# Moving small reciprocals from VectorE to GpSimd, and two small VectorE operations one place later, in a top-32 attention with mixture of depths

## The chip, the cores and the metric

The kernel runs on one core of a Trainium2 chip. The metric is the device time in microseconds (us) of one execution; a core has five engines with queues of their own: PE (TensorE), DVE (VectorE), ACT (ScalarE), POOL (GpSimd) and SP (SyncE, here only DMA).

## The reference

Inputs q, k and v are float32 of shape (8, 8, 576, 64): batch, heads, rows, width. The mixture has w_gate (512), w1 (512 x 1024), w2 (1024 x 512) and a capacity of 128. Cut to what matters:

```python
scores = (q @ k.T) / 8                                # 576 x 576 for each batch and head
kth    = 32nd largest score of each row
scores = where(scores >= kth, scores, -1e9)
e      = exp(scores - row max)
x      = (e / (sum(e) + 1e-9)) @ v                    # heads side by side: (8, 576, 512)
s      = x @ w_gate                                   # one gate a token
top    = the 128 tokens of a batch with the largest s
ye     = relu(x[top] @ w1) @ w2
out    = x;  out[top] += ye / (1 + exp(-s[top]))
```

## The kernel before, in words

**Units and steps.** The work is cut into 144 units, 18 for each of the 8 batches. A unit is a tile of 128 query rows for two heads (four tiles of four units a batch), or the last 64 rows for four heads (two units a batch). One loop, `for n in range(-1, N)` at L1192, runs all units as a pipeline: in step n the scores of unit n+1 are multiplied, the search of unit n is begun, that of unit n-2 ended, and unit n-4 is weighed and multiplied by v. Everything is recorded through `InOrder` (L38 to L46), so each engine executes in the order of the program text, and the profile gives L46 as the line of nearly all instructions; tiles tell them apart.

**The 32nd score.** ACT copies the scores from PSUM to the tile `sc`. DVE takes the eight largest of each of seven pieces of a row into `cand` (`find_bound`, L544: 14 MAX8 a step, for two heads), and from these candidates the 24th (`best`, `bound`). ACT takes the signs of score minus bound (`sides`, L578), POOL multiplies score by sign (`y<-sc,sides`, L1160, two a step), and DVE takes the eight largest of that (`next<-y`, `find_kth`, L598); the last of them is the 32nd. `mask` (L603) marks the smaller scores in `less`: head 0 by ACT, head 1 by POOL. PE transposes scores and marks together, ACT takes the exponential (`pT`, `last`), PE multiplies by v and a column of ones, and ACT copies the result to `xs`, and the sums plus 1e-9 to `sums` (`keep_sums`, L735).

**Dividing by the sums.** In the step after a tile's last unit, `normalise` (L730) calls `divide` (L738). DVE takes the reciprocal of 8 sums of a row into `rden`, and POOL multiplies `xs` by it into `x`. The call is put at the front of `vector_late` (L1225), which `find_bound` empties between the two heads (L552). So DVE has the reciprocal between its 7th and its 8th MAX8 of `cand`, and POOL has the multiplication between its mask of that step and the two `y` of that step. One step later DVE takes the dot product with w_gate (`dot`, L1028). There are 40 tiles; the very last is divided by lines of its own (L1447).

**The mixture.** `mixture` (L786) is a generator, whose pieces run in chosen steps of the next batch (`mix_at`, L1072). `multiply_places` finds the chosen tokens by PE; `add_up` (L895) adds parts (`place`), makes row numbers (`row_i`, by `keep_rows`) and the gates (`g`), all by DVE at the end of a step, out of the list `after_kth`. A POOL DMA fetches the rows in the next step. ACT takes exp(-g), and `squash` (L906) makes 1/(1+g) by two DVE instructions, out of `vector_late`. ACT uses `g` much later, in `gy`. `keep_least` (L1174) takes the least 32nd score of a batch by a DVE reduction of `next`, recorded in the step that follows the batch's last `find_kth`, ahead of that step's MAX8.

**What sets the order.** Lists of closures: `late` and `copies_late` for ACT, `vector_late` and `amid_late` for DVE, `pool_late` for POOL (emptied after `find_bound`, L1307), `after_kth` for DVE after `find_kth`. The last units have a hand-written order from L1335 on. `general` (L1655) and `general_weights` are a slower way for other inputs, taken only where `is_unsure` is set, and the profiled execution does not run them.

Of the kernel before, what the change touches and what calls it, by code (L numbers as in the profile page):

```python
# [11 lines left out]
ALU = mybir.AluOpType  # L12
FP32 = mybir.dt.float32
# [36 lines left out]
def kernel(  # L50
# [11 lines left out]
    nc = tc.nc  # L62
    P = nc.NUM_PARTITIONS
    B, H, S, D = q.shape
# [14 lines left out]
    const = ctx.enter_context(tc.tile_pool(name="const", bufs=1))  # L79
# [3 lines left out]
    wkpool = ctx.enter_context(tc.tile_pool(name="wk", bufs=2))  # L83
# [3 lines left out]
    modpool = ctx.enter_context(tc.tile_pool(name="mod", bufs=1))  # L87
# [32 lines left out]
    for i in range(2):  # L120
# [22 lines left out]
    least = const.tile([P, B], FP32, name="least")  # L143
    bounded = const.tile([P, NS], FP32, name="bounded")
    sums = const.tile([P, B * NT, H], FP32, name="sums")
    nc.gpsimd.memset(sums, 1.0)

    MIDDLE = S - 2 * (TOP_K - 8) + 1
    steps_i = const.tile([P, 2, 8], I32, name="steps_i")
# [16 lines left out]
        out=slot_signs,  # L166
        in0=slot,
        scalar1=-2.0,
        scalar2=float(S - 1),
        op0=ALU.mult,  # L170
# [22 lines left out]
    def load_weights():  # L193
# [6 lines left out]
    pe, dve, act, pool, sp = (  # L200
        InOrder(tc, e)
        for e in (nc.tensor, nc.vector, nc.scalar, nc.gpsimd, nc.sync)
    )
# [16 lines left out]
    late, vector_late, pool_late = [], [], []  # L220
# [3 lines left out]

    kept, values_bank = [], [None]

    after_kth = []

    def flush_copies():
        while copies_late:  # L230
# [2 lines left out]
    def flush():  # L233
        flush_copies()
        while late:
            late.pop(0)()
# [307 lines left out]
    def find_bound(sc, bound):  # L544

        cand = wkpool.tile([P, 2, 8 * PARTS], FP32, name="cand")
        best = [stats.tile([P, 2, 8], FP32, name=f"best{r}") for r in range(2)]
        best.append(bound)
        for i in range(2):

            if i == 1:
                flush_vector()  # L552
            for u in range(PARTS):
                if (i, u) == (1, 2) and amid_late:
                    amid_late.pop()()
                dve.max(
                    cand[:, i, 8 * u : 8 * u + 8],
                    sc[:, i, u * S // PARTS : (u + 1) * S // PARTS],
                )


        parts = cand.rearrange("p i (u e) -> p i u e", u=PARTS)
        for r, e in enumerate((3, 7, 8)):
            for i in range(2):
                dve.max(best[r][:, i, :], parts[:, i, :, 0:e])
            if r < 2:
                for i in range(2):
                    dve.match_replace(
                        parts[:, i, :, 0:e],
                        best[r][:, i, :],  # L570
                        parts[:, i, :, 0:e],
                        LOWEST,
                    )
# [163 lines left out]

    def divide(n, xs, x, den):  # L738
        rden = stats.tile([P, H], FP32, name="rden")
        dve.reciprocal(out=rden[0:n, :], in_=den)  # L740
        pool.tensor_tensor(
            x.rearrange("p (h d) -> p h d", h=H),
            xs[0:n, :, 0:D],
            rden[0:n, :].unsqueeze(2).to_broadcast([n, H, D]),
            ALU.mult,
        )
# [39 lines left out]
    def mixture(row0, pg, rank, exact=False, sign_sum=None):  # L786
# [8 lines left out]
        if exact:  # L795
            for t0, t1, at in ((0, J, 0), (J, NT, JP)):
                tr = ps_misc.tile([P, 512], FP32, name="tr", tag="misc")
                n = R if t0 else P
# [8 lines left out]
        else:  # L807
            row_dram = drampool.tile([1, S], FP32, name="row_dram")
            sp.dma_start(
                out=row_dram[0, R * NT : S].rearrange("(p j) -> p j", j=J),  # L810
                in_=gate[R:P, 0:J],
            )
            sp.dma_start(
                out=row_dram[0, 0 : R * NT].rearrange("(p j) -> p j", j=NT),
                in_=gate[0:R, 0:NT],
# [18 lines left out]
        for t in range(NT):  # L834
            yield
            n = R if t == J else P
# [52 lines left out]
        g = modpool.tile([P, 1], FP32, name="g", bufs=2)  # L889
# [4 lines left out]

        def add_up():  # L895
            add_parts(place, found)
            keep_rows(
                place,
                row_i,
                row0 if isinstance(row0, float) else row0[:, 0:1],  # L900
                float(done * S - 1),
            )
            dve.tensor_scalar_max(out=g, in0=place[:, 1:2], scalar1=-88.0)
            late.append(lambda: act.activation(g, g, AF.Exp, scale=-1.0))

        def squash():  # L906
            dve.tensor_scalar_add(out=g, in0=g, scalar1=1.0)
            dve.reciprocal(out=g, in_=g)

        kept.append(lambda: after_kth.append(add_up))  # L910
        if exact:
            for todo in (kept, after_kth):
                while todo:
                    todo.pop(0)()
        yield
# [15 lines left out]
        for fc in range(NFC):  # L931
            yield
            if fc == 1:
                vector_late.append(squash)
            if fc % 2 == 0:
                ps = ps_misc.tile([P, 2, CAP], FP32, name="h_ps", tag="misc")
            multiply_h(ps[:, fc % 2, :], fc, xeT)
            if fc % 2 == 1:
                copies_late.append(
                    lambda ps=ps, fc=fc: act.activation(  # L940
                        hT[:, fc - 1 : fc + 1, :], ps, AF.Relu
                    )
                )
# [34 lines left out]
    def add_parts(place, found):  # L978
        dve.tensor_reduce(
            out=place,  # L980
            in_=found[:, 0:6].rearrange("p (a e) -> p a e", e=3),
            axis=mybir.AxisListType.X,
            op=ALU.add,
        )

    def keep_rows(ps, row_i, row0, most):

        dve.tensor_scalar(
            out=row_i,
            in0=ps[:, 0:1],  # L990
            scalar1=row0,
            scalar2=most,
            op0=ALU.add,
            op1=ALU.min,
        )
# [99 lines left out]
    for b in range(B - 1):  # L1095
        n = (b + 1) * per_batch + mix_at_of.get(b, mix_at)[6]
# [77 lines left out]
    def keep_least(b, bound, kth):  # L1174
        at = 2 * per_batch * b
        late.append(
            lambda: act.copy(
                out=bounded[:, at : at + 2 * per_batch].rearrange("p (n i) -> p n i", i=2),
                in_=bound,
            )  # L1180
        )
        dve.tensor_reduce(
            out=least[:, b : b + 1], in_=kth, axis=mybir.AxisListType.XY, op=ALU.min
        )

    def mask_of(n, on=None):
# [5 lines left out]
    for n in range(-1, N):  # L1192
        b, i = divmod(n, per_batch)
# [48 lines left out]
        if is_unit(n + 1):  # L1242
            b, t, g = units[n + 1]
# [15 lines left out]
        if is_unit(n + 1) and n + 1 >= NHP:  # L1259
            b, i = divmod(n, per_batch)  # L1260
# [56 lines left out]
        if gating is not None:  # L1317
            b, t = gating
# [10 lines left out]
        b, i = divmod(n, per_batch)  # L1329
# [117 lines left out]
    rden = stats.tile([P, H], FP32, name="rden")  # L1447
# [20 lines left out]
    for t in (0, 1):  # L1468
        pool.tensor_scalar(
            out=pick[:, t, :],  # L1470
            in0=slot,
            scalar1=rank[:, t : t + 1],
            scalar2=others[:, t : t + 1],
            op0=ALU.subtract,
# [8 lines left out]
    for t in (J - 1, J):  # L1483
        n = R if t == J else P
        dve.tensor_scalar(
            out=pick[0:n, t, :],
            in0=slot[0:n, :],
            scalar1=rank[0:n, t : t + 1],
            scalar2=others[0:n, t : t + 1],
            op0=ALU.subtract,  # L1490
# [5 lines left out]
    g = modpool.tile([P, 1], FP32, name="g", bufs=2)  # L1496
# [15 lines left out]
    for i in range(2):  # L1512
        dve.tensor_scalar(
            out=half_i[:, i : i + 1],
            in0=row_i,
            scalar1=2.0,
            scalar2=float(i),
            op0=ALU.mult,
# [10 lines left out]
    for copy, half, dc in zip((act.copy, dve.tensor_copy), halves, (0, 2)):  # L1529
        copy(  # L1530
            out=xeT[:, dc : dc + 2, :],
            in_=half[:, 0 : 2 * CAP].rearrange("p (c i) -> p c i", c=2),
        )

    keep_least(B - 1, bounds.pop(B - 1)[:, :, :, 7], next8s.pop(B - 1)[:, :, :, 7])
    flush()
    low = modpool.tile([P, S], I32, name="low", tag="scratch")[:, 0:NS]
    dve.tensor_scalar(
        out=low,
        in0=bounded.bitcast(I32),  # L1540
        scalar1=(1 << 23) - 1,
# [85 lines left out]
    def general_weights(sc):  # L1627

        p = wkpool.tile([P, 2, S], FP32, name="p", tag="y")
        for i in range(2):  # L1630
            cur, tops = sc[:, i, :], []
            left = wkpool.tile([P, 2, S], FP32, name="left", tag="y")
            for r in range(TOP_K // 8):
                tops.append(stats.tile([P, 8], FP32, name=f"top{r}", bufs=2))
                nc.vector.max(tops[-1], cur)
                if r < TOP_K // 8 - 1:
                    nc.vector.match_replace(left[:, 0, :], tops[-1], cur, LOWEST)
                    cur = left[:, 0, :]
            shift = stats.tile([P, 1], FP32, name="shift", bufs=2)
            nc.vector.tensor_scalar_mul(shift, tops[0][:, 0:1], -scale)  # L1640
            e = wkpool.tile([P, S], FP32, name="e", tag="sides")
            nc.scalar.activation(
                e, sc[:, i, :], AF.Exp, bias=shift, scale=scale
            )
            nc.vector.scalar_tensor_tensor(
                out=p[:, i, :],
                in0=sc[:, i, :],
                scalar=tops[-1][:, 7:8],
                in1=e,
                op0=ALU.is_ge,  # L1650
                op1=ALU.mult,
            )
        return p
# [77 lines left out]
```

## Time and profile before

| | |
|---|---|
| Median of 3 runs | 786.59 us (786.38 to 789.53) |
| The profiled execution | 788.9 us, of which 786.6 us from its first to its last instruction (the span) |
| Granted TensorE clock | 0.996 |
| Busy: PE, DVE, ACT, POOL | 725.7, 756.7, 731.3, 692.4 us |
| DVE RECIPROCAL of `rden` | 40, 188 ns each with 128 rows, 180 ns with 64 |
| DVE RECIPROCAL of `g` | 8, 164 ns each |
| POOL `x<-xs,rden` | 39, about 1.04 us each |
| DVE reductions of `next` to `least` | 8, 217 ns each |

"Busy" is time in which an engine has at least one instruction between its start and its end. On DVE the next instruction starts before the one in front of it has ended, so durations of small instructions, added up, give more than they occupy; the distance from one start to the next tells what one occupies. A wait is put down to the engine and the tile that released it last.

### The profile page before, as it was taken

To read this page: it belongs to the slowest core of one execution; us is meant where nothing else is said; L and a number is where in the kernel's file an instruction comes from. 1 tells how busy PE (TensorE), PEld (TensorE's weight loads), DVE (VectorE), ACT (ScalarE), POOL (GpSimd) and SP (SyncE) were. 2 spreads that over 40 slices of the span, in tenths; PEclk is the share of its full clock that TensorE was granted. 3 is DMA by queue.
4 is the path that set the end of the run, shared out by engine and by line. 5 is a ranking of instruction groups with operands and counts; after the bars stand their busy time and mean duration, and the time that the engine had idled before them with its cause. 6 is when DMAs were issued, how large, how long until landed. Compare 5 with 4: busy or idle time off the path is not lost. (4 is left out here: it accounts for less than half of the span.)

```text
span 786.6 us, 33176 instructions
## 1 busy us (share of the span) xinstructions
PE 725.7 (92%) x12535; PEld 550.5 (70%) x12535; DVE 756.7 (96%) x4602; ACT 731.3 (93%) x1535; POOL 692.4 (88%) x732
## 2 busy tenths in 40 slices
PE   8888888888999989999999999999899989999987
PEld 6766666666786668766786667866687658757756
DVE  7999999999999999999999999999999999999952
ACT  6999999999999999999999999999999999989730
POOL 3899999999999998999999999999999999999821
PEclk9999999999999999999999999999999999999899
DMA  8941215121151132321251221512233102101021
GB/s 168 293 105 39 48 56 111 30 55 30 62 118 35 38 94 54 76 57 42 70 110 31 56 43 63 114 26 50 65 77 82 30 15 70 25 15 17 2 75 31
DMA packets 121751, 50.69 MB, mean 64 GB/s; under 512 B 116016, under 2 KB 116016, under 8 KB 120560
## 3 DMA queue, kind: packets, MB, share of 16 engines
q1 hardware_dynamic: 118368, 43.94, 22.7%
q0 software_dynamic: 1744, 4.20, 3.0%
q8 instruction: 101, 1.65, 0.9%
q14 instruction: 66, 0.54, 0.2%
q10 hardware_dynamic: 1472, 0.36, 0.2%
HBM read 36.93 MB, written 11.55 MB: 62 GB/s over the span
## 5 line engine op out<-in xcount | busy, mean ns | idle before, releaser
L46 POOL TENSOR_TENSOR y<-sc,sides 128x576 f32<-128x576 f32 x288 | 349.8, 1237 | 24.8 <-ACT sides L46 23.3
L46 DVE MAX8 cand<-sc 128x8 f32<-128x82 f32 (+1 forms) x2016 | 313.1, 230 | 3.0 <-ACT sc L46 2.9
L46 POOL TENSOR_SCALAR less<-sc,next 128x576 bf16<-128x576 f32 x135 | 233.3, 1728 | 28.4 <-DVE next L46 23.8
L46 ACT ACTIVATE sides<-sc,bound 128x576 fp8e4<-128x576 f32 x288 | 230.9, 802 | 3.9 <-DVE bound L46 3.7
L46 PEld LDWEIGHTS av<-v,pT 128*64 128x64 f32 x4608 | 146.9, 138 | 87.2 <-ACT last L46 78.7
L46 DVE MAX8 next<-y 128x8 f32<-128x584 f32 x288 | 204.4, 751 | 0.0
L46 PE MATMUL av<-v,pT 128*64 128x65 f32 x4608 | 166.9, 225 | 35.0 <-ACT last L46 34.7
L46 PE MATMUL ps<-kT,qT 64*128 64x288 f32 (+1 forms) x1248 | 170.4, 422 | 2.9 <-ACT sc L46 2.1
L46 PEld LDWEIGHTS <-less 64*128 64x128 bf16 (+1 forms) x2448 | 161.2, 131 | 13.0 <-POOL less L46 10.0
L46 PE MATMUL ptr<-ident,sc 64*128 64x64 f32 x2272 | 161.5, 253 | 0.0
L46 ACT COPY sc<-ps 128x1152 f32<-128x1152 f32 x140 | 160.5, 1146 | 0.0
L46 ACT ACTIVATE pT<-ptr 128x1024 f32<-128x1024 f32 x142 | 147.3, 1037 | 10.1 <-PE ptr L46 9.3
L46 PEld LDWEIGHTS ptr<-ident,sc 64*128 64x128 f32 x2272 | 138.2, 137 | 23.8 <-issue 23.7
L46 PE MATMUL ptr<-out_of_reach,less 64*128 64x64 bf16 x2272 | 148.2, 190 | 6.3 <-POOL less L46 5.3
L46 ACT ACTIVATE less<-sc,next 128x576 bf16<-128x576 f32 x147 | 115.4, 789 | 0.0
L46 PEld LDWEIGHTS ps<-kT,qT 64*128 64x128 f32 (+1 forms) x1248 | 92.6, 176 | 22.6 <-ACT sc L46 5.1
L46 DVE MATCH_REPLACE8 cand<-best,cand 128x21 f32<-128x21 f32 (+1 forms) x576 | 99.0, 180 | 0.0
L46 DVE MAX8 best<-cand 128x8 f32<-128x21 f32 (+1 forms) x576 | 91.0, 191 | 0.0
L46 ACT ACTIVATION_READ_ACCUMULATOR sides<-sc,bound 128x1 f32 x288 | 63.6, 221 | 0.0
L46 PE MATMUL h_ps<-xeT,w 128*128 128x128 f32 x464 | 61.9, 278 | 0.0
L46 PEld LDWEIGHTS av<-ident,sc 128*128 128x128 f32 x144 | 20.0, 139 | 55.9 <-issue 40.9
L46 PE MATMUL av<-vpair,last 128*64 128x130 f32 x576 | 56.9, 276 | 0.0
(167 smaller groups left out, 916.2 us busy)
## 6 DMA issues: line engine op xcount, KB each, us to landing
v<-in_v_dram SPq DMA_DIRECT2D x64, 128.0 KB, 4.0
out_dram<-x SPq DMA_DIRECT2D x8, 1024.0 KB, 3.9
rows<-in_k_dram SPq DMA_DIRECT2D x56, 128.0 KB, 2.9
rows<-in_q_dram SPq DMA_DIRECT2D x56, 128.0 KB, 3.1
w<-in_moe_w_dram SPq DMA_DIRECT2D x2, 2048.0 KB
gate_row<-row_dram SPq DMA_DIRECT2D x7, 288.0 KB, 4.6
last<-in_q_dram SPq DMA_DIRECT2D x8, 128.0 KB, 3.5
vpair<-in_v_dram SPq DMA_DIRECT2D x16, 64.0 KB, 5.1
```

Of the source, the lines that this page charges most:

```text
L46: return lambda *a, **kw: self._tc.keep_in_program_order(fn(*a, **kw))
```

## The change

The 39 reciprocals of `divide` and the two operations of `squash` go from DVE to POOL, as a sum with an immediate and powers of -1, with a tile of -1 as the second operand. `squash` goes into `pool_late` and so runs after `find_bound` of the same step. The reduction in `keep_least` and, of `add_up`, all but the first addition go into a new list `after_max`, emptied after the first MAX8 of `cand` in the next `find_bound`: the same step's for the reduction, the next step's for row numbers and gates. The exponential of `g`, which `use_place` puts into `late`, runs one step later for that. A tile of the other way, `general_weights`, moves to another pool. The last tile's reciprocal (L1448) and the last batch's gate (L1509) stay on DVE.

```diff
+    minus_one = const.tile([P, H], FP32, name="minus_one")
+    nc.gpsimd.memset(minus_one, -1.0)
...
-    after_kth = []
+    after_kth, after_max = [], []
...
                     cand[:, i, 8 * u : 8 * u + 8],
                     sc[:, i, u * S // PARTS : (u + 1) * S // PARTS],
                 )
+                while after_max:
+                    after_max.pop(0)()
...
     def divide(n, xs, x, den):
         rden = stats.tile([P, H], FP32, name="rden")
-        dve.reciprocal(out=rden[0:n, :], in_=den)
+        pool.tensor_tensor(rden[0:n, :], den, minus_one[0:n, :], ALU.pow)
...
         def add_up():
             add_parts(place, found)
+            after_max.append(use_place)
+
+        def use_place():
             keep_rows(
...
         def squash():
-            dve.tensor_scalar_add(out=g, in0=g, scalar1=1.0)
-            dve.reciprocal(out=g, in_=g)
+            pool.tensor_scalar(
+                out=g, in0=g, scalar1=1.0, scalar2=None, op0=ALU.add
+            )
+            pool.tensor_tensor(g, g, minus_one[:, 0:1], ALU.pow)
...
-            for todo in (kept, after_kth):
+            for todo in (kept, after_kth, after_max):
...
             if fc == 1:
-                vector_late.append(squash)
+                pool_late.append(squash)
...
-        dve.tensor_reduce(
-            out=least[:, b : b + 1], in_=kth, axis=mybir.AxisListType.XY, op=ALU.min
+        after_max.append(
+            lambda: dve.tensor_reduce(
+                out=least[:, b : b + 1], in_=kth, axis=mybir.AxisListType.XY, op=ALU.min
+            )
         )
...
     keep_least(B - 1, bounds.pop(B - 1)[:, :, :, 7], next8s.pop(B - 1)[:, :, :, 7])
+    after_max.pop()()
...
-            e = wkpool.tile([P, S], FP32, name="e", tag="sides")
+            e = modpool.tile([P, S], FP32, name="e", tag="scratch")
```

## The prediction

> **What bounds the kernel now.** First the busy times of the page and of one batch in the middle of the loop (18 units), from a view of stretches: us, then the busy us of PE, PEld, DVE, ACT and POOL with instructions in brackets.
>
> ```profile
> PE 725.7 (92%) x12535; PEld 550.5 (70%) x12535; DVE 756.7 (96%) x4602; ACT 731.3 (93%) x1535; POOL 692.4 (88%) x732
> ...
> 100.00:745.00 645.00, 606.49 (x10726) 459.22 (x10724) 644.20 (x3944) 630.31 (x1318) 603.42 (x615) 1.00 0.24 55
> ...
> 398.00:490.30 92.30, 88.76 (x1557) 66.78 (x1555) 92.20 (x568) 91.28 (x193) 86.46 (x89) 1.00 0.27 63
> ```
>
> DVE has 0.10 us of idle time in a batch of 92.30 us: it bounds the loop, and the page's 96% comes from the two ends. But ACT has only 92.30 - 91.28 = 1.02 us left in a batch, POOL 92.30 - 86.46 = 5.84 us. A DVE saving counts as far as these two can follow. Who waits for whom in that batch (engine, tile, what it waits for; us in total, times, longest), for ACT and then POOL:
>
> ```profile
> ACT pT L46 <- PE ptr L46: 0.4, 1, 0.4
> ACT sides L46 <- DVE bound L46: 0.3, 1, 0.3
> ...
> POOL less L46 <- DVE next L46: 3.2, 5, 0.7
> POOL y L46 <- ACT sides L46: 1.3, 3, 0.6
> ```
>
> No row has DVE as the waiting engine. POOL's idle time is mostly waiting for DVE's `next`, so it shrinks when DVE is faster, and it is POOL's room for new work.
>
> **What a small DVE instruction occupies** is read from starts in the timeline (start, us, engine, operation, tiles, count). A step without a reciprocal, one with, and the places of `squash` and of the two moved operations:
>
> ```profile
> 406.25 2.12 DVE L46 MAX8 cand<-sc 128x8 f32<-128x82 f32 x14
> 408.28 0.30 DVE L46 MAX8 best<-cand 128x8 f32<-128x21 f32 x2
> ...
> 410.99 1.10 DVE L46 MAX8 cand<-sc 128x8 f32<-128x82 f32 x7
> 412.01 0.18 DVE L46 RECIPROCAL rden<-sums 128x8 f32<-128x8 f32 x1
> 412.11 1.07 DVE L46 MAX8 cand<-sc 128x8 f32<-128x82 f32 x7
> 413.09 0.30 DVE L46 MAX8 best<-cand 128x8 f32<-128x21 f32 x2
> ...
> 379.35 1.42 DVE L46 MAX8 next<-y 128x8 f32<-128x584 f32 x2
> 380.80 0.22 DVE L46 TENSOR_REDUCE least<-next 128x1 f32<-128x36 f32 x1
> ...
> 386.76 0.14 DVE L46 TENSOR_SCALAR g<-g 128x1 f32<-128x1 f32 x1
> 386.93 0.16 DVE L46 RECIPROCAL g<-g 128x1 f32<-128x1 f32 x1
> 387.01 0.37 DVE L46 MAX8 cand<-sc 128x8 f32<-128x82 f32 x2
> ...
> 365.54 0.14 DVE L46 TENSOR_REDUCE place<-places 128x2 f32<-128x6 f32 x1
> 365.72 0.15 DVE L46 TENSOR_SCALAR row_i<-place 128x1 int32<-128x1 f32 x1
> 365.79 0.14 DVE L46 TENSOR_SCALAR g<-place 128x1 f32<-128x1 f32 x1
> ```
>
> Fourteen MAX8 take 408.28 - 406.25 = 2.03 us, and with the reciprocal between them 413.09 - 410.99 = 2.10 us: a reciprocal costs 0.07 us, not its 0.18.
>
> **What the Trainium skill says.** "VectorE: DVE Perf Modes", section "The DRAIN you can't avoid": a VectorE instruction that reads what the one in front of it wrote is safe only with a semaphore wait or with another VectorE instruction between them. The trace agrees that such a wait costs: `place` to `row_i` is 0.18 us, while `row_i` to `g` (no such reading) is 0.07. "GPSIMD Engine Reference", section "Performance pitfalls for Q7 kernels": a chain of dependent float32 operations takes 4 cycles an element for each of them, unless independent ones are interleaved; section "Specifications": the clock is 1.2 GHz. No run here shows that yet, and no page prices a power. "Perfetto Trace Analysis", section "GPSIMD Engine Instruction": GpSimd work is to be timed from start to start; I do so with the small chain below.
>
> **The change, part by part.** *Taken from DVE.* Reciprocals of sums: 39 x 0.07 = 2.7 us (the 40th stays). `squash`: 387.01 - 386.76 = 0.25 us, seven times (the last batch's stays): 1.75 us. *Moved on DVE.* The reduction of `next` starts 380.80 - 379.35 = 1.45 us after the two MAX8 it reads began; two such MAX8 in front of something else take 1.33 us (404.92 to 406.25). So 0.12 us is the wait for the result; one MAX8 between (2.03/14 = 0.145 us) is longer than that and hides it: 7 x 0.12 = 0.84 us. Row numbers: `place` to `row_i` 0.18, less the roughly 0.06 that such a reduction would occupy by itself (estimate from the 0.07 of `row_i`): 0.12 us, seven times: 0.84 us. A batch saves 5 x 0.07 + 0.25 + 0.12 + 0.12 = 0.84 us; all of it 2.7 + 1.75 + 0.84 + 0.84 = **6.1 us**.
>
> *Given to POOL.* The shape nearest to the power of 128 x 8 in the trace is the subtraction of 128 x 5, and the chain of which it is part shows a wait of one POOL instruction for the one before:
>
> ```profile
> 403.47 0.20 POOL L46 CAST parts<-gate 128x5 bf16<-128x5 f32 x1
> 403.76 0.20 POOL L46 TENSOR_TENSOR rest<-gate,parts 128x5 f32<-128x5 f32 x1
> ...
> L46 POOL TENSOR_TENSOR y<-steps,seen 128x16 f32<-128x16 f32 x144 | 33.3, 231 | 0.0
> ```
>
> So a small instruction takes 0.20 us, and one that waits for it starts 0.29 us after it, 0.09 more; 16 elements take 0.23. If a power took no longer than a subtraction, p = 0.21 us. That is the lower bound; nothing in the trace bounds it above. By the page, each dependent operation of a power costs 8 elements x 4 cycles / 1.2 GHz = 0.027 us at worst. I take **p = 0.35 us** (estimate: 0.20 and some six such operations, or many more interleaved); the range goes to about 1.05. A batch adds to POOL five powers and their waits, 5(p + 0.09), and in one step sum, wait and power of the gate, 0.20 + 0.09 + p (a whole p, though it has one element): 6p + 0.74 us, at p = 0.35 2.8 us. Within a batch of 92.30 - 0.84 = 91.46 us POOL's room is 91.46 - 86.46 = 5.0 us: it fits, up to p = 0.71.
>
> *Who waits for that.* Behind the power stand the product `x`, two `y`, the fill and the next mask on POOL. Nothing arrives late for it: `sums` was ready at 409.95 (ACT, 409.73 for 0.22), `x` began at 413.20. `x` ended at 414.24 and its dot product began on DVE at 417.11: 2.9 us of cover for p + 0.09. The `y` of a step are read by `next` one step later: the fill ended at 407.29, `next` began at 409.65, 2.4 us of cover. The mask is read by PE at once (in this batch PE's transposes wait for it 0.2 us), then comes ACT's `pT`, then the copy `sc`; but `sc` is there 1.3 us or more before the first MAX8 that reads it (408.40 for 410.99 in the step shown), so a mask that is 0.4 us late uses up lead, not time. If that lead is gone, DVE waits for `cand<-sc`.
>
> *Costed at nothing.* The row numbers come some 0.3 us into the next step; the fetch by POOL stands behind that step's mask of 1.7 us. The exponential of `g` one step later, and the gate after it on POOL: `gy` uses it many steps later. The 32-byte tile, the other pool for `e` (never run). SP and PE keep their order; POOL's two indirect DMAs a batch are not moved, only what stands ahead of them grows by p.
>
> *The ends.* In the hand-written end the reciprocal (751.16) to `x` (751.44) is 0.28 us; power and wait are 0.35 + 0.09 = 0.44: +0.2 us, as DVE's dot product waits for `x` there. ACT has 1.02 - 0.84 = 0.18 us left in a batch; its 0.3 us for DVE's `bound` goes away, its 0.4 for PE may stay in some: I give back 0.3 us. Sum: -6.1 + 0.5 = -5.6 us. The profiled execution was 788.9 us (span 786.6), so 783.3 for it; it stands 2.3 above the median of the runs, 786.59, and against that the number is **781.0 us**.
>
> **The rivals.** *ACT becomes the bound.* For it: 1.02 us of idle time a batch, of which the saving needs 0.84, and the waits for PE. Against it: ACT leads DVE by 1.3 us at the least, and an ACT that loses its lead stops waiting. If 0.6 us of waits stay, the batch is 91.9 us: over 7.5 batches 3.0 us gained, 783.6. The two moves hiding nothing (1.7 us less) would come out near it, at 782.7. Together 0.11.
>
> *POOL becomes the bound, slower.* The power is a long program on POOL. Then 6p + 0.74 fills POOL's 5.84 us: from p = 0.85 the gain is gone, and each 0.1 us more costs 0.6 us a batch, 4.5 us in all. At p = 1.0: 0.9 x 7.5 = +6.8, 793.4 us; at 1.2: 2.1 x 7.5 = +15.8, 802.4 us. For it: POOL is busy 94% of the batch, and no page prices a power; 0.85 us is reached with 24 dependent operations that are not interleaved, (0.85 - 0.20)/0.027. Against it: only eight elements a row. 0.23.
>
> **How the numbers follow.** Forecast (p below 0.7, ACT follows): 0.66, 781.0 us, its own range 779.5 to 782.5. About 0.5%, 3.9 us, is what a measurement of this kernel can tell from no change: faster is below 782.7, slower above 790.5. The ACT case lies within: same 0.11; POOL: slower 0.23. The low end, 779.2, has 0.10 us for a reciprocal instead of 0.07, and nothing given back. For 8 in 10 the high end takes in POOL up to p of about 1.05: 796.
>
> **What would show it.** Right: DVE still without idle time in a batch of about 91.5 us, POOL's power below 0.5 us from its start to that of `x`, POOL's wait for `next` down from 3.2 us by some 2, no gap between `next` and the reduction of `least`. Wrong: rows in which DVE waits for POOL's `y` or ACT's `sc`; a power of 0.9 us or more; ACT without idle time and DVE with some.

## The result: 858 us, slower by 9%

| | before | after |
|---|---|---|
| Median | 788.36 us (6 runs, 786.38 to 789.53) | 858.29 us (6 runs, 856.07 to 862.98) |
| Ratio to before | | 1.090 (1.0875 to 1.0924) |
| Span of the profiled execution | 786.6 us | 861.2 us |
| Dot products with w_gate on DVE, 40 | 32.5 us | 66.0 us |

The forecast was 781.0 us; the change cost 70 us. The granted TensorE clock was 0.970 in the profiled execution, 0.996 before. Kernels below that lose 17 and 25 us kept 0.995, so a loss of that size needs no lower clock; what a lower clock adds to the larger losses was not tested. First the page of the changed kernel and one of its batches (us, then busy us of PE, PEld, DVE, ACT and POOL):

```profile
PE 753.1 (87%) x12535; PEld 567.0 (66%) x12535; DVE 792.4 (92%) x4549; ACT 734.0 (85%) x1535; POOL 779.4 (90%) x786
...
437.00:538.90 101.90, 92.14 (x1549) 68.71 (x1549) 97.20 (x561) 91.75 (x194) 97.75 (x96) 0.97 0.25 57
```

A batch went from 92.30 to 101.9 us. POOL's busy time in it rose from 86.46 to 97.75. More surprising, DVE, from which work was taken, is busy 35.7 us longer over the span, with 53 instructions fewer. The costs of the new work, by shape (group, count, then busy us, mean ns of one):

```profile
L46 POOL TENSOR_TENSOR rden<-sums,minus_one 128x8 f32<-128x8 f32 x32 | 53.4, 1669 | 3.3 <-ACT sums L46 3.3
...
L46 POOL TENSOR_TENSOR g<-g,minus_one 128x1 f32<-128x1 f32 x7 | 4.3, 618 | 0.6
```

A power of 8 numbers a row takes 1.67 us, of one number 0.58 (six of the seven; the seventh, 0.87, lay beside a dot product, and the mean is 0.62): some 0.16 us a number and 0.42 us fixed, if it is a straight line. From the power's start to that of the product `x` it is 1.75 us (454.01 to 455.76 in the timeline). Where the engines of the changed kernel wait (engine, tile, what it waits for; us in total, times, longest):

```profile
ACT pT L46 <- PE ptr L46: 73.9, 69, 3.5
...
PE ptr L46 <- POOL less L46: 61.0, 38, 2.8
...
POOL y L46 <- ACT sides L46: 35.3, 27, 15.3
...
DVE cand L46 <- ACT sc L46: 20.8, 21, 3.5
DVE prod L46 <- POOL x L46: 15.5, 24, 1.7
```

The late POOL mask is now what PE waits for (5.3 us before), ACT waits for PE, and DVE at the end of that chain waits for scores. POOL itself still waits for ACT's `sides`, although it is late: it is one link of a ring, and the others do not run on without it.

The longer DVE time sits in one operation. The timeline around one dot product, DVE and then POOL:

```profile
434.25 2.87 DVE L46 CUSTOM_DVE_ANT_0 prod<-x,wg 64x512 f32<-64x512 f32 x1 [1.37 <-POOL x L46]
437.05 0.07 DVE L46 DVE_READ_ACCUMULATOR2_ANT gate<- 64x1 f32 x1
```

```profile
431.44 1.66 POOL L46 TENSOR_TENSOR rden<-sums,minus_one 64x8 f32<-64x8 f32 x1
433.18 1.04 POOL L46 TENSOR_TENSOR x<-xs,rden 64x512 f32<-64x512 f32 x1
434.18 2.39 POOL L46 TENSOR_TENSOR y<-sc,sides 128x576 f32<-128x576 f32 x2
436.54 0.66 POOL L46 TENSOR_TENSOR y<-steps,seen 128x16 f32<-128x16 f32 x1
437.18 1.72 POOL L46 TENSOR_SCALAR less<-sc,next 128x576 bf16<-128x576 f32 x1
```

The dot waits 1.37 us for `x`, starts the moment `x` is there, and so runs beside what follows `x` on POOL: the two products `y` and the fill (`y<-steps,seen`, 16 numbers a row), all with two inputs. It takes 2.87 us instead of 0.69, and ends only where POOL's fill (0.66 us instead of 0.21) ends and the one-input mask begins. The same tile over each kernel's whole execution (minimum, median and maximum ns), before and after:

```profile
L46 DVE CUSTOM_DVE_ANT_0 prod<-x,wg x40: 674/694/1593, 50.7 to 756.9; 128x512 f32<-128x512 f32 x32, 64x512 f32<-64x512 f32 x8
```

```profile
L46 DVE CUSTOM_DVE_ANT_0 prod<-x,wg x40: 673/1680/2878, 55.9 to 831.6; 128x512 f32<-128x512 f32 x32, 64x512 f32<-64x512 f32 x8
```

Before, nearly every dot lay beside POOL's mask (36 of the 40 began beside it). The Trainium skill says in "GPSIMD Engine Reference", section "Specifications", that GpSimd's SBUF interfaces are shared with VectorE, with contention against VectorE instructions "with two SBUF inputs". The dot is one, and the trace agrees that it is slow there, 2.87 us. The prediction used that page for the cost of a power and passed over this line. The experiments ask whether it is a cause, and how much of the 70 us it makes.

### The profile page after: what moved, and what is told of

Its sections match the earlier page's. It is cut to its first block, busy times and chain, and to the rows that moved or that the text cites. A ratio compares the mean times of both kernels' runs of the same rounds, so it can differ in the third digit from the quotient of the medians.

```text
span 861.2 us, 33100 instructions
## 1 busy us (share of the span) xinstructions
PE 753.1 (87%) x12535; PEld 567.0 (66%) x12535; DVE 792.4 (92%) x4549; ACT 734.0 (85%) x1535; POOL 779.4 (90%) x786
## 5 line engine op out<-in xcount | busy, mean ns | idle before, releaser
L46 POOL TENSOR_TENSOR y<-sc,sides 128x576 f32<-128x576 f32 x288 | 364.1, 1288 | 40.8 <-ACT sides L46 35.3
L46 DVE MAX8 cand<-sc 128x8 f32<-128x82 f32 (+1 forms) x2016 | 312.5, 229 | 22.1 <-ACT sc L46 20.8
L46 ACT ACTIVATE sides<-sc,bound 128x576 fp8e4<-128x576 f32 x288 | 227.0, 788 | 0.1
L46 ACT ACTIVATE pT<-ptr 128x1024 f32<-128x1024 f32 x142 | 145.3, 1023 | 74.0 <-PE ptr L46 73.9
L46 PE MATMUL ps<-kT,qT 64*128 64x288 f32 (+1 forms) x1248 | 178.9, 437 | 3.2 <-ACT sc L46 2.9
L46 PE MATMUL ptr<-ident,sc 64*128 64x64 f32 x2272 | 163.5, 253 | 0.0
L46 PEld LDWEIGHTS ps<-kT,qT 64*128 64x128 f32 (+1 forms) x1248 | 96.2, 180 | 23.1 <-ACT sc L46 4.5
L46 DVE CUSTOM_DVE_ANT_0 prod<-x,wg 128x512 f32<-128x512 f32 (+1 forms) x40 | 66.0, 1651 | 15.6 <-POOL x L46 15.5
L46 POOL TENSOR_TENSOR rden<-sums,minus_one 128x8 f32<-128x8 f32 (+1 forms) x39 | 65.0, 1667 | 3.3 <-ACT sums L46 3.3
L46 PE MATMUL h_ps<-xeT,w 128*128 128x128 f32 x464 | 66.1, 290 | 0.0
L46 PEld LDWEIGHTS h_ps<-xeT,w 128*128 128x128 f32 x464 | 60.4, 204 | 0.6
```

The lines of the kernel that those rows point to most:

```text
L46: return lambda *a, **kw: self._tc.keep_in_program_order(fn(*a, **kw))
```

## The experiments

**Theory.** Three things add up: (1) a power is 1.75 us of POOL's time; (2) POOL has too little room for that, and the ring POOL mask - PE - ACT - POOL and DVE slows; (3) the dot product, bound to the end of `x`, slides from POOL's one-input mask onto its two-input products. **Rivals:** a power harms other engines in a way of its own; the long dots are only a form of waiting, and the missing room is the whole loss.

### Which part of the change

Both powers back on DVE, only the moves left (`moves_only`):

```diff
-        pool.tensor_tensor(rden[0:n, :], den, minus_one[0:n, :], ALU.pow)
+        dve.reciprocal(out=rden[0:n, :], in_=den)
...
+            dve.tensor_scalar_add(out=g, in0=g, scalar1=1.0)
+            dve.reciprocal(out=g, in_=g)
...
-                pool_late.append(squash)
+                vector_late.append(squash)
```

> The changed kernel with both powers put back as DVE reciprocals: only the reduction of the least scores and the row numbers stand behind the first MAX8. Both theories (POOL's room, and DVE's dot product running into POOL's products) say that these moves have no part in the loss: 0.12 us for each of 14 places, 1.7 us, so a ratio to before of 0.998 (0.996 to 1.000). Its trace should show no gap between MAX8 of next and the reduction of least.

Measured: 785.05 us, ratio 0.9962 (0.9949 to 0.9976): about 3.0 us faster. The timeline of DVE there:

```profile
378.32 1.42 DVE L46 MAX8 next<-y 128x8 f32<-128x584 f32 x2
379.65 0.23 DVE L46 MAX8 cand<-sc 128x8 f32<-128x82 f32 x1
379.80 0.20 DVE L46 TENSOR_REDUCE least<-next 128x1 f32<-128x36 f32 x1
```

Two MAX8 of `next` take 1.33 us to the next start, and the reduction follows one MAX8 of 0.15 us later: the wait is gone. The gain is at or a little over the forecast 1.7 us, whose ratio 0.9978 lies just outside the interval. Where the rest comes from is open; the other pool for `e` came with it.

The gate's power too on POOL, the sums on DVE (`moves_gate`):

```diff
-        pool.tensor_tensor(rden[0:n, :], den, minus_one[0:n, :], ALU.pow)
+        dve.reciprocal(out=rden[0:n, :], in_=den)
```

> The changed kernel with the sums' reciprocals back on DVE; the gate's sum and power stay on POOL (0.20 + 0.09 + 0.62 us, seven times in all, 0.9 us a batch of POOL's 5.8 us of idle time). Room theory: it fits, so 1.75 us less than with the moves alone, ratio to before 0.996 (0.993 to 0.998). If a power slows other engines whatever its length (rival), it is slower than the moves alone by 1 us or more.

Measured: 785.89 us, ratio 0.9966 (0.9955 to 0.9977): nothing gained over the moves. DVE was rid of 1.75 us, but its dots took 35.6 us in all against 32.2 with the moves alone. Nearly all of them still lay beside POOL's mask, but many began nearer to its start; what that does is seen below with `work_350`.

The kernel before with the powers of sums alone (`sums_only`), with the gate's in addition (`sums_gate`), and with the moves in addition (`sums_moves`):

```diff
-        dve.reciprocal(out=rden[0:n, :], in_=den)
+        pool.tensor_tensor(rden[0:n, :], den, minus_one[0:n, :], ALU.pow)
...
```

> The kernel before with nothing but the 39 reciprocals of sums as powers on POOL. Both theories: nearly the whole loss is here, ratio to before 1.085 to 1.10, with the dot products of DVE at 1.2 to 2.9 us instead of 0.7 to 1.0.

> The sums' powers and the gate's sum and power on POOL, none of the moves. POOL is full with the sums' powers (844 us), so the gate's 0.9 us a batch should come on top in full: 0.9 x 7 = 6 us, 850 us (847 to 855). If the gate is free also then, 843.

> The sums' powers and the two moves, the gate on DVE. By the changed kernel (858) less the gate's 6 us: 852 us. If the moves keep their gain of 3 us with POOL full: 841. A value over 846 says that a faster DVE only waits longer for x (17 waits, 7.5 us with the sums alone; 24 waits, 15.5 us in the changed kernel).

Measured: 844.35 us, ratio 1.072 (1.0694 to 1.0746); 856.95, 1.086 (1.0834 to 1.0886); 850.83, 1.0774 (1.0744 to 1.0803). Most of the loss, 56 of 70 us, is the powers of sums; the first expectation was too high. The gate, nearly free with the sums on DVE, costs 13 us with POOL full, twice its own 6 us. The moves, good for 3 us alone, cost about 6 there (and about 1 once the gate is on POOL as well, 858.29 against 856.95). With the moves, dots waited 8.6 us for `x` (20 times) instead of 7.5 (17 times), and DVE waited 15.6 us for scores instead of 6.1. The expectation had put their cost down to the wait for `x`; it is mostly the wait for scores.

### A power, or any work of that length

The kernel before, with work on POOL at the power's place that nobody reads, of 1.73, 0.93 and 0.34 us (`work_1700`, `work_900`, `work_350`; k is 96, 43, 4):

```diff
         dve.reciprocal(out=rden[0:n, :], in_=den)
+        pool.tensor_scalar(
+            out=burn,                       # 128 x 6k, bf16
+            in0=ident[:, 0:k].unsqueeze(1).to_broadcast([P, 6, k]),
+            scalar1=slot[:, 0:1],
+            scalar2=None,
+            op0=ALU.is_lt,
+        )
...
```

> The kernel before, with reciprocals on DVE, and on POOL at the power's place a comparison of 128 x 576 numbers with one input that nobody reads (about 1.7 us, 38 to 39 times). If the time of a power matters and not that it is a power, about what the sums' powers alone gave, 844 us (833 to 855), with dots of 1.2 us and more. If a power harms other engines in a way of its own, well below: 805 to 825.

> The same with 258 numbers, about 0.93 us. The rule of the prediction: a batch's POOL room of 5.8 us holds five of these (4.7 us), so ratio 0.999 to 1.004. If the order within the step counts before the room is used up (the dot product sliding from the mask onto the products y), slower: 1.008 to 1.03, with some dots over 1.2 us.

> The kernel before, with a POOL comparison of 24 numbers at the power's place, about 0.35 us: the duration that the prediction assumed for a power. DVE keeps its reciprocals, so no gain is due. Room rule: 5 x 0.35 = 1.75 us of 5.8 us a batch, ratio 0.998 to 1.002, and the forecast would have held with such a power. If dots slide onto y already, 1.003 to 1.01: then the forecast's 5.6 us would have been lost even so.

| POOL work at the place | measured | ratio to before | 40 dots |
|---|---|---|---|
| none | 788.6 us | 1 | 32.5 us |
| 0.34 us | 793.66 us | 1.006 (1.0039 to 1.0081) | 37.4 us |
| 0.93 us | 806.10 us | 1.0215 (1.0178 to 1.0252) | 50.6 us |
| 1.73 us | 846.41 us | 1.0724 (1.0685 to 1.0762) | 79.1 us |

The longest gives about what the powers gave (844 us): it is POOL's time that costs, not the power, and the first rival falls. The other two fell in the direction that the room rule had excluded: 5 and 17 us are lost where the room, 5.8 us a batch, takes 1.7 and 4.6. Both losses are as large as what the dots grew by, 4.9 and 18.1 us, and DVE's idle time stayed what it was (span less busy time: 29.9 us before, 29.7 and 31.0). The dots with 0.34 us of POOL work:

```profile
L46 DVE CUSTOM_DVE_ANT_0 prod<-x,wg x40: 672/1002/1905, 51.0 to 760.9; 128x512 f32<-128x512 f32 x32, 64x512 f32<-64x512 f32 x8
```

The median dot is 1.00 us instead of 0.69. With 0.93 us of work, 32 of the 40 dots began beside a product `y`. With 0.34 us it was not `y` that they met: 33 still began inside a mask, which has one input. What changed is how long the mask had been running. A mask and its dot, before and with 0.34 us of work:

```profile
489.17 1.72 POOL L46 TENSOR_SCALAR less<-sc,next 128x576 bf16<-128x576 f32 x1
...
489.76 0.69 DVE L46 CUSTOM_DVE_ANT_0 prod<-x,wg 64x512 f32<-64x512 f32 x1
```

```profile
492.75 1.71 POOL L46 TENSOR_SCALAR less<-sc,next 128x576 bf16<-128x576 f32 x1
...
493.02 1.00 DVE L46 CUSTOM_DVE_ANT_0 prod<-x,wg 64x512 f32<-64x512 f32 x1
```

One dot begins 0.59 us after its mask, the other 0.27 us, and both end 1.27 to 1.28 us after the mask's start. In these two kernels 51 dots begin like this in the first 0.6 us of a mask, and all end 1.27 to 1.32 us after its start; the 18 that begin later take 0.67 to 0.68 us. (One more begins together with its mask and takes 0.67 us; that mask takes 2.27 us.) So the mask too holds a dot up, in its first 0.6 us, and the third point of the theory, in which the mask was harmless, is wrong there. Nor was POOL work found here that is free because there is room for it: a mask that comes 0.3 us later changes what the dots meet.

### The dot beside two-input work

In the kernel before, the dot later in its step, POOL without any new work (`dot_on_y`):

```diff
-                if (i, u) == (1, 2) and amid_late:
-                    amid_late.pop()()
...
                         LOWEST,
                     )
+            if r == 0 and amid_late:
+                amid_late.pop()()
```

> The kernel before with one edit: the dot product of x with w_gate stands about 1.2 us later in the same VectorE step (behind the first two MATCH_REPLACE8 instead of between the MAX8), where POOL is in its two-input products y instead of its one-input mask. POOL gets no work. Theory of the shared SBUF interface: the dots rise from 0.7 to 1.0 us to 1.2 to 2.9 us and the kernel is 25 to 40 us slower, ratio 1.03 to 1.05. Rival (the long dots of the changed kernel are only a sign of waiting, not a cost): dots as before, ratio 0.999 to 1.003.

Measured: 813.95 us, ratio 1.0316 (1.028 to 1.0352), 25 us. The dots grew by 30.8 us to 63.4:

```profile
L46 DVE CUSTOM_DVE_ANT_0 prod<-x,wg x40: 676/1253/3517, 52.1 to 786.6; 128x512 f32<-128x512 f32 x32, 64x512 f32<-64x512 f32 x8
```

The place alone makes them long, and the time is lost. Not each dot in that place is long. Some that begin shortly before the product take 0.68 us, and then the product is the longer one (at 144.04 us: the dot 0.68, the `y` beside it 1.67 instead of 1.21).

Then three kernels that move something in the changed kernel: the power and `x` behind the products `y` (`power_behind_y`); that, and the dot a step later (`dot_two_later`); the dot a step later alone (`dot_later`).

```diff
-            vector_late.insert(0, lambda a=inverting: normalise(*a))
+            behind_y.append(lambda a=inverting: normalise(*a))
...
             weigh_signs(n - 1)
+        while behind_y:
+            behind_y.pop(0)()
```

> The changed kernel with the power and the product x put behind the step's two products y on POOL instead of ahead of them, so that what follows x on POOL is the mask (one input) and not y (two inputs). The work of POOL is the same. If room alone costs the time, it stays near 858 us (850 to 865). If the dot product of DVE, which starts when x is ready, is slow because POOL runs the two-input y beside it, the dots fall back to 0.7 to 1.0 us and the kernel comes to about 825 us (815 to 835), the rest being POOL's missing room.

```diff
-    mix_at = (5, 7, 9, 10, 13, 14, 16, 16, *range(19, 36))
+    mix_at = (6, 7, 9, 10, 13, 14, 16, 16, *range(19, 36))
...
-        gating = normalised
+        gating = done_before
+        done_before = normalised
...
```

> The kernel of the power behind y, with the dot product (and the store and the mixture's first pieces) one step later, so that the dot neither waits for x nor stands beside y. POOL's work is that of the changed kernel. What is left is POOL's room: 9.7 us of new work a batch against 5.8 us, 3.8 x 7.5 = 29 us more than before, 817 us (810 to 830). If the loss has another cause (the mask late for PE by the power in front of it), it stays above 840.

> The changed kernel with one thing moved: the dot product with w_gate (and with it the store and the first pieces of the mixture) stands one step later. Powers, products and masks keep the order of the changed kernel. In the changed kernel dots took 33.5 us more than before and waited 15.5 us for x. If these two are the loss beyond POOL's room, the kernel comes down from 858 to 805 to 822 us, dots at 0.7 to 1.1 us and no wait for x. If the late mask (PE waits 61 us for it) is what costs, it stays at 840 or more.

Measured: 894.76 us, ratio 1.1348 (1.1327 to 1.1369); 861.38, 1.0927 (1.0883 to 1.0972); 842.89, 1.0695 (1.0666 to 1.0725). The first missed both of its forecasts; the other two missed the lower one and came out where a late mask was to be the cause. Behind `y` the dots were short, 27.6 us in all, but 38 of them began at the start of a mask, and these masks took 2.25 to 2.27 us instead of 1.72: POOL paid in their place. And `x` came so late that the dots waited for it:

```profile
DVE prod L46 <- POOL x L46: 106.1, 39, 3.8
```

I had not counted that the dot follows `x` by one step in the program and POOL was late already. With the dot a step later that wait is 2.6 us and the dots 38.4 us, but the power now stands ahead of the mask; PE waited 66.1 us for the mask, DVE 39.4 us for scores and 23.1 us for `y`. With the dots near their old length, the waits alone can cost that much. In `dot_later` the wait for `x` went from 15.5 to 1.7 us and that for scores from 20.8 to 7.5, while DVE waited 24.8 us for `y` instead of 2.7; the dots stayed on `y` (58.7 us instead of 66.0), and 15 us of time were gained. None of the three separates the parts.

The last pair comes nearer. It leaves the order alone and takes the dot's second SBUF input away (`one_input_after`, and in the kernel before `one_input_before`; w_gate is left out, so other tokens are picked):

```diff
-        dve.tensor_tensor_reduce(out=prod[0:n, 0:HD], in0=x, in1=wg[0:n, :], ...)
+        dve.tensor_scalar(out=prod[0:n, 0:HD], in0=x, scalar1=wg[0:n, 0:1],
+            scalar2=None, op0=ALU.mult, op1=ALU.add, accum_out=g)
```

> The changed kernel with the dot product of x and w_gate replaced by a sum of x times one number: a VectorE instruction of the same place and number of elements that reads one SBUF tensor, not two. It leaves out w_gate, so the mixture picks other tokens, as many. If the second SBUF input is what makes the dots long beside POOL's y, they fall from 1.7 us to about 0.7 us and the kernel loses about those 33 us, to 825 us (818 to 835); what is left over before is POOL's room with the mask late for PE, and the wait for x. If the dots stay long, the second input is not the cause; if they get short and the time stays over 845, DVE's lost time was only a wait in another place.

> The same replacement in the kernel before (w_gate left out as there). Its dots took 32.5 us for 40; without the excess over 0.68 us they would take 27: ratio 0.992 to 1.000. A larger gain would say that the replacement is cheaper by itself, and take that off the first run's difference.

Measured: 828.71 us, ratio 1.0509 (1.047 to 1.0549), and 783.19 us, ratio 0.9941 (0.9914 to 0.9967). The tile in the first, and what DVE waits for there:

```profile
L46 DVE TENSOR_SCALAR_CACHE_REDUCE prod<-x,wg x40: 723/738/748, 52.5 to 802.3; 128x512 f32<-128x512 f32 x32, 64x512 f32<-64x512 f32 x8
```

```profile
DVE cand L46 <- ACT sc L46: 26.6, 34, 3.1
DVE prod L46 <- POOL x L46: 18.1, 25, 1.7
```

All forty take 0.72 to 0.75 us in the changed kernel's order, still waiting for `x` in 25 cases, and nearly all still beside `y`. In `one_input_before` they take 0.72 to 0.75 us too, also where they begin in the first 0.6 us of a mask. So the meeting is what makes the dots long, and the replacement that reads one tensor does not have it. (The replacement is also another instruction; that the number of inputs decides, and not the kind of instruction, agrees with the page named above, but was not tested by itself.)

In the changed kernel the long dots cost 858.3 - 828.7 = 29.6 us; the replacement is worth 787.8 - 783.2 = 4.6 us in the kernel before, where 13 dots that began in the first 0.4 us of a mask took 0.9 to 1.05 us. What the change costs without the contention is 828.7 - 783.2 = 45.5 us, so contention made about 70 - 45 = 25 us of the loss and POOL's missing room, with what follows from it, 45. In the 25 lies also what the dots cost POOL: products `y` and fills took 400.3 us in the changed kernel and 384.6 with one input. In the 45 lie two waits of DVE that the kernel before hardly has: 26.6 us for scores, behind POOL's late mask and the ring (2.9 in `one_input_before`), and 18.1 us for `x` (none there).

## Why the prediction was wrong, point by point

- **What bounds the kernel:** right. DVE had almost no idle time in the loop, and where DVE is relieved and POOL gets no work (`moves_only`), time is gained. Whether ACT follows the whole saving of 0.84 us a batch stays open; no kernel here had it.
- **The moves, 1.7 us:** right in mechanism; measured 3.0 us (1.9 to 4.0).
- **The price of a power, p = 0.35 us:** the first step that failed, a term of the sum that was sized too small. It measured 1.67 us, and 1.75 to the next start. The prediction had no upper bound from trace or page, and a range up to 1.05 us was a guess about a program that no page describes. The 128 x 1 power is 0.58 us, not a whole p.
- **POOL's room, "each 0.1 us more costs 0.6 us a batch":** the rival "POOL becomes the bound" named the right side, with a chance of 0.23. Its own rule, with the measured prices, gives 5 x 1.75 + 0.29 + 0.62 = 9.7 us a batch against 5.84, and 3.8 x 7.5 = 29 us, 815 to 817 us. It is short by over 40 us for two reasons. It let new work use all of POOL's idle time; in the batch shown POOL still idles 101.9 - 97.75 = 4.15 us, so only 1.7 of 5.84 were used: the mask is late for PE, and ACT, behind PE, is late for POOL. And it kept the rest of POOL's work at its length, while products and fill, slowed by the dots, took some 1.6 us more a batch: 97.75 - 86.46 - 9.7.
- **"`x` ended at 414.24 and its dot product began at 417.11: 2.9 us of cover":** the second step that failed. It failed as cover: POOL fell behind by more than 2.9 us, and the dot waited for `x` 24 times, 15.5 us in all. And it was cover against waiting only. What the dot meets on POOL at its place, and how long it takes there, was put at nothing without being asked, and that is where about 25 us came from.
- **If p had been 0.35:** 0.34 us of work cost 5 us in `work_350`, about all of the forecast gain of 5.6. So the kernel would have come out near no change even with the forecast's own price (an estimate from these two numbers); the rule of room fails well before the room is used, because 0.34 us is enough to move dots into the first 0.6 us of a mask.
- **The signs of being wrong that it named:** they came. DVE waits for ACT's `sc` (20.8 us), and the power is over 0.9 us.
- **The end, 0.2 us; the costs of nothing:** not tested by themselves; nothing in the runs points to them.

Of the kernels here that use w_gate, `moves_only` is the fastest: the two VectorE operations behind a MAX8, with reciprocals and gate on VectorE, 785.05 us. `moves_gate`, 785.89 us, is level with it within the intervals.

## What to carry to other kernels

Before work is moved to an engine that has idle time, ask for each instruction of the full engine that shares a memory interface with it what will run beside it afterwards. Here a two-input VectorE operation was fast because it began in the later part of a GpSimd operation; 0.3 us of new GpSimd work moved it into the first part and cost 5 us, and 1.7 us moved it onto two-input products. The idle time of POOL, a link in a ring of waits, was not room. And an operation that neither the trace nor a page prices is measured by itself first.

## What was not expected of the hardware

- GpSimd's power: 1.67 us for 128 x 8 (64 x 8 the same, 1.66), 0.58 us for 128 x 1, where a subtraction of 128 x 5 takes 0.20.
- The dot product, a VectorE operation with two SBUF inputs (0.67 to 0.69 us for 512 numbers a row), took 2.87 us when it began with a GpSimd product of two inputs, and ended with the fill behind two such products; that fill took 0.66 instead of 0.21 us. The replacement with one input took 0.74 us at the same place.
- GpSimd's mask, with one input, held such a dot up only in the mask's first 0.6 us of 1.72: of 69 dots of the kernel before and `work_350`, those that began there ended 1.27 to 1.32 us after the mask's start, and later ones took 0.67 us.
- Either of the two can be the one held up: of the dots that began within 0.07 us of a mask's start, some took 0.67 to 0.69 us, and their masks 2.21 to 2.29 instead of 1.72; others took 1.22 to 1.24, and their masks 1.71 to 1.73.
